# Group 1's first dense layer by seven products in all four units, under a new order of all operations (attention with squared ReLU, then two dense layers)

## The chip, the cores and the metric

The kernel runs on one core of one Trainium2 chip. The metric is the device time of one execution in microseconds (us). The kernel before took 365.93 us in the median of three runs (365.68 to 366.21). One execution was profiled: it took 365.47 us, and its span, from the first to the last instruction, is 363.7 us at a mean granted TensorE clock of 0.999.

## What is computed

```python
scores = (1 / sqrt(64)) * q @ k.T                  # 8 batches x 12 heads, 448 x 448, depth 64
attn_out = (max(scores, 0)**2 / 448) @ v           # per head: 448 x 64
x = attn_out as 3584 rows of 768                   # heads side by side
h = x @ w_in                                       # 3584 x 768 times 768 x 2048: first dense layer
g = h * sigmoid(1.702 * h)
out = g @ w_out                                    # 3584 x 2048 times 2048 x 768: second dense layer
```

Inputs and output are float32. Inside, matrix operands are float16 and sums are float32 in PSUM. The scale factors are held back and applied inside the GELU and at the output copies.

## The kernel before

**Attention.** The work is cut into 24 attention units of four heads of one batch (three units per batch). A unit's q and k are loaded, cast to float16 and transposed (the first six units by TensorE, the others by a DMA transpose). For each of seven blocks `j` of keys, `scores` (L143) issues four matmuls that run side by side in the four 64x64 quarters of the array and write two PSUM banks. `relu` (L156) copies each bank to SBUF with a ReLU, on ScalarE (L163) or VectorE (L161). `square` (L165) squares the two halves in one instruction, on ScalarE (L169) or VectorE (L88). `attn_v` (L173) multiplies by v in 28 matmuls. `xt_evac` (L189) copies the result to the transposed input of the dense layers, `xe` or `xo`.

**Dense layers.** The 3584 rows are taken in eight groups of 384 (even groups) and 512 (odd groups) rows. The first layer of a group gives sixteen tiles of 128 of the 2048 hidden columns. There are two ways to compute them:

- Plain: `m1` (L221) computes one tile `f` by six matmuls as wide as the group, two per call (words `f<g>.<f>.<r>`). Then `m1_gelu` (L233) reads PSUM on ScalarE and `m1_widen` (L238) scales into the float16 tile `ge`/`go` on GpSimd or VectorE.
- Seven products: `unit_product` (L269) handles a unit `i` of four hidden tiles at once. It splits weights and input into 2x2 blocks and needs seven block products in place of eight (a Strassen-Winograd scheme). Each product (word `u<g>.<i>.<n>`) is six matmuls of half the group's width. The sums of the input blocks (`t_sum`, L259, words `T`) are made once per group, those of the weight blocks (`s_sum`, L245, words `S`) once per unit for the whole kernel, both on VectorE. Two PSUM banks hold a unit. The first is copied out after products 0, 2 and 4 (`unit_snap`, L288, words `t`, on ScalarE or VectorE); the second is added to such a copy after products 1, 3 and 6 (`unit_add`, L295, words `b`, on VectorE). Four GELUs (`unit_gelu`, L299) and four scalings (`unit_widen`, L307) follow, each over two half tiles.

Group 0 is plain, groups 2 to 7 use seven products, and group 1 uses `m1` for hidden tiles 0 to 7 (the words `f1.0` to `f1.7`) and seven products for its units 2 and 3. The second layer (words `p`, `pair_product`, L375) uses seven products on pairs of row blocks and `single` (L399) on the odd block of the even groups; its block sums are the words `A` and `W` on VectorE. Stores go out on SyncE's queue.

**The order.** Nothing is scheduled at build time. The string `words` (L467 to L640) is a list of 1950 words, one per operation, written by a planner outside the kernel, and `do` (L441) issues them one after the other. Each engine takes its own operations in the order of this list. A suffix `:a`, `:d` or `:p` puts an operation on ScalarE, VectorE or GpSimd, and `@` names PSUM banks. Semaphores follow from the data and buffers.

The few lines that matter for the change:

```python
for i in (2 * r, 2 * r + 1):                                   # m1, L228
    nc.tensor.matmul(out=hp[g, f][:, 0:n], lhsT=w[:, i, fo:fo + 128],
                     rhs=xts[g][:, i, 0:n], start=i == 0, stop=i == NK - 1)
...
for t in range(2):                                             # unit_product, L269
    mm(hx[g, i, c][:, t * hn:(t + 1) * hn],
       lambda j: a[:, j, t * 128:(t + 1) * 128], lambda j: b[:, j, :], HK,
       n in (0, 1, 3) and t == 0)
```

All weight loads are DMAs issued by GpSimd (`jwa`, `jwb`, `jo`), as are the loads of v and of the first q and k; later q and k loads and transposes are on SyncE's queue.

Of the kernel before, what the change touches and what calls it, by code (L numbers as in the profile page):

```python
# [15 lines left out]
def kernel(  # L16
# [406 lines left out]
    with tc.manual_schedule():  # L423
# [35 lines left out]
        def zeros(e, p, n):  # L459
# [8 lines left out]
            "jq1 z13@0 z1 jk1 I jwb2 Lq0 Q0:a tq0@1 Lk0 jq2 K0:d tk0@2 eq0 ek0 jk2 tq1@3 eq1 "  # L468
            "s0.2@4.5 s0.3@6.7 tk1@0 r0.2.1 V0 r0.3.0 r0.3.1:d ek1 r0.2.0 s0.5@1.2 r0.5.0 s0.1@3.5 "
            "r0.1.0:d s0.0@6.7 r0.0.0 r0.5.1:d r0.1.1 jk3 s0.4@0.4 s0.6@1.3 r0.6.1:d r0.6.0 "  # L470
            "s1.0@6.2 r1.0.1 r1.0.0 r0.4.0 V1 r0.0.1:d s1.2@5.3 r0.4.1:d jq3 x0.6:a jwb0 r1.2.0 "
            "x0.5 s1.1@1.2 r1.1.1 x0.4 s1.5@6.0 r1.5.0:d x0.0 r1.5.1 jwa0 r1.2.1:d s1.3@7.4 x0.3 "
            "r1.1.0 x0.2 s1.4@5.2 x0.1:a tq2@6 x1.0 tk2@0 eq2 x1.5:a jk4 a0@3.1 ek2 r1.3.0 e0.1.0 "
            "jq4 s1.6@6.0 V2 jwa2 tk3@7 x1.1:a e0.0.0 r1.4.0 jwb1 r1.4.1:d ek3 s2.0@3.5 x1.4 "
            "e0.0.1:a tq3@2 jwa1 r1.3.1 x1.3 r2.0.1 jk5 s2.4@7.4 r1.6.0 r2.4.0 jq5 V3 e0.1.1 "
            "r2.4.1:d jwb3 s2.1@5.6 x1.2 r1.6.1 x1.6 s2.2@7.1 r2.0.0 a1@4.0 jwa3 r2.2.1 V4 r2.1.0 "
            "r2.2.0 r2.1.1 V5 x2.0 e1.0.0:a eq3 e1.1.0 s2.6@3.1 e1.0.1:a x2.1 jo1.0 r2.6.0 e1.1.1 "
            "s2.3@5.7 s2.5@6.2 r2.3.0 r2.3.1:d x2.2 r2.5.1 jo0.0 f0.3.0@4 f0.3.1 r2.6.1:d s3.3@3.0 "
            "s3.2@5.7 r3.2.1:d r3.3.1 r3.3.0 tk4@2 r2.5.0:d tq4@1 x2.3:a ek4 jo1.1 r3.2.0 x2.4 "
            "f0.2.0@7 x2.5:a x2.6 f0.2.1 s3.0@0.3 a2@6.2 r3.0.1 e2.0.1:a e2.1.0:a eq4 s3.1@5.3 "  # L480
            "r3.1.0 e2.1.1:a e2.0.0 jo0.1 r3.1.1:d x3.1 f0.1.0@1 f0.1.1 f0.1.2 x3.2 f0.3.2 r3.0.0 "
            "f0.2.2 g0.1 g0.3 v0.3:d f0.0.0@5 v0.1:d g0.2 s3.5@2.6 s3.6@3.0 r3.6.0 s3.4@1.4 r3.6.1 "
            "r3.4.1 r3.4.0:d f0.8.0@7 f0.8.1 f0.0.1 r3.5.1 r3.5.0:d f0.0.2 x3.4 v0.2 f0.8.2 "
            "s4.2@3.0 g0.0 r4.2.1:d x3.3:a s4.3@4.1 s4.1@6.2 r4.1.1 x3.5 r4.1.0 f0.6.0@5 f0.6.1 "
            "r4.3.0 x3.0 f0.6.2 g0.6 f0.4.0@0 f0.4.1 f0.4.2 g0.8 r4.3.1:d r4.2.0:d s4.4@2.6 "
            "r4.4.0:d tk5@4 x3.6 r4.4.1 tq5@5 g0.4 v0.4 s4.0@7.1 eq5:a ek5 s4.5@3.2 G3 a3@6.0 "
            "s5.6@5.4 r4.5.1 r4.0.0:d r4.5.0 x4.4 x4.2:a e3.0.0 s5.0@2.7 f0.7.0@3 r5.0.1:d r5.6.0:d "
            "r5.0.0 Lk6 f0.7.1 x4.1:a f0.10.0@6 r4.0.1 Lq6 f0.10.1 f0.10.2 g0.10 v0.10 f0.5.0@7 "
            "f0.5.1 f0.5.2 g0.5 K6:p e3.0.1:a Lk7 f0.7.2 f0.11.0@5 v0.6:d f0.11.1 r5.6.1 s5.1@2.1 "
            "r5.1.0 s4.6@6.7 f0.11.2 r5.1.1 f0.15.0@0 r4.6.0 v0.0:d x4.0 f0.15.1 x4.3 f0.15.2 g0.7 "  # L490
            "r4.6.1:d s5.4@4.2 x4.5 r5.4.1 x4.6 a4@1.6 r5.4.0:d s5.5@3.7 g0.11 s5.3@2.4 g0.15 "
            "e4.0.1:a s5.2@5.0 v0.15 r5.5.1:d x5.0:a f0.13.0@6 f0.13.1 f0.13.2 r5.5.0:d r5.3.0 x5.4 "
            "Rk6 x5.5:a V6 f0.9.0@7 S3.1 v0.8 e4.0.0 f0.9.1 r5.3.1 f0.14.0@3 v0.5 f1.4.0@2 f0.9.2 "
            "S3.2 f0.14.1 f0.14.2 g0.13 v0.7 V8 g0.9 r5.2.0:d f0.12.0@1 f0.12.1 S0.1 f0.12.2 V7 "
            "f1.1.0@4 v0.9 r5.2.1 v0.11 f1.4.1 f1.7.0@6 g0.14 v0.14 x5.2 f1.7.1 x5.3:a u1.3.0@7 "
            "x5.6 T1.1 x5.1:a a5@5.0 f1.1.1 g0.12 t1.3.0 Q6:d S1.1 e5.0.1:a u1.2.0@3 S2.1 Lq8 S2.2 "
            "f1.0.0@1 e5.0.0:a f1.1.2 S2.4 v0.12:d t1.2.0 f1.4.2 S1.2 T1.2 v0.13 S2.3 Rq6 g1.4 T1.4 "
            "A0.0.1@0 u1.2.1@0 b1.2.1 W0.1 f1.0.1 f1.3.0@5 f1.3.1 f1.3.2 W2.1 A0.0.3 f1.2.0@2 S3.3 "
            "u1.3.2 g1.1 g1.2.1 v1.1 f1.5.0@4 f1.5.1 v1.2.1 K7 f1.2.1 g1.3 f1.2.2 Lk8 W1.1 g1.2 "
            "f1.5.2 S3.4 A0.0.2@1 f1.7.2 g1.5 v1.2:d u1.2.2 v1.3 g1.7 f1.0.2 g1.0 v1.5 v1.4 t1.2.2 "  # L500
            "f1.6.0@5 t1.3.2 f1.6.1 T1.3 p0.0.0@2 W3.1 v1.0:d f1.6.2 u1.2.4 Q8:a t1.2.4 W0.2 u1.2.3 "
            "h0.0.0 v1.7:d W2.2 u1.3.4 W0.3 b1.2.3 g1.6 u1.2.5 W2.3 v1.6:d Lq7 g1.2.3 v1.2.3 "
            "s6.0@4.6 r6.0.0 W1.2 s6.2@1.5 u1.2.6 u1.3.1@4 r6.2.0:d Rk7 W3.2 b1.3.1 r6.0.1 Rq8 W3.3 "
            "W1.3 g1.2.5 s6.1@1.6 p0.0.1@3 r6.1.0 W0.4 t1.3.4 x6.0:a g1.3.1 u1.3.5 u1.3.3 r6.1.1:d "
            "l0.0.1 r6.2.1 p0.0.2 b1.2.6 x6.2:a b1.3.3 Q7:a Rq7 h0.0.2:d s6.5@1.6 r6.5.0:d r6.5.1 "
            "v1.3.1 s6.3@5.0 r6.3.1:d g1.3.5 K8:p x6.1:a v1.3.5 Lq9 Q9 u1.3.6 b1.3.6 g1.3.6 v1.3.6 "
            "Lk9 K9:p p0.0.4 h0.0.4 s6.4@1.6 r6.4.1 W3.4 r6.3.0 W2.4 r6.4.0 s6.6@0.7 r6.6.0 W1.4 "
            "A0.0.4 v1.2.5 p0.0.3 r6.6.1:d p0.0.5 x6.4 x6.5:a s7.2@4.6 l0.0.3 r7.2.0 r7.2.1 x6.3 "
            "Rk8 s7.0@5.1 r7.0.1:d r7.0.0 g1.2.6 l0.0.5 s7.1@0.7 r7.1.1:d p0.0.6 x6.6:a l0.0.6 Lq10 "
            "s7.3@4.6 A0.2.5@1 r7.1.0 r7.3.1 o0.1 r7.3.0:d a6@1.5 Lk11 e6.1.1 e6.1.0 e6.0.1:a "  # L510
            "s7.6@2.7 x7.2 r7.6.0 r7.6.1 Q10 e6.0.0:a s7.4@3.0 r7.4.0:d p1.0.0@6 s7.5@4.5 Rq9 "
            "r7.4.1 s8.1@2.7 r7.5.1 r8.1.0 s8.0@1.3 r8.0.1 x7.3 r7.5.0:d r8.0.0 x7.1:a Rk9 x7.6:a "
            "K11:p i0.2.0@0 s8.6@5.2 r8.6.0 x7.0 x7.5 r8.6.1 x8.6:a r8.1.1:d x7.4 n0.2.0 x8.1 "
            "a7@3.4 e7.1.0:a e7.0.0:a Lk10 Lq11 v1.2.6 s8.2@1.5 e7.1.1:a S1.4 s8.3@2.7 x8.0:a K10:p "
            "r8.2.0:d e7.0.1 A1.0.1@0 r8.2.1:d i0.2.1@0 r8.3.1 A1.0.3 r8.3.0 Rk11 A1.0.2@1 h1.0.0 "
            "n0.2.1:a p1.0.1@3 x8.3:a V9 o0.2 s8.4@1.4 s8.5@5.7 r8.4.0 r8.4.1 r8.5.1 x8.2 Q11 "
            "r8.5.0:d s9.2@2.0 Lk12 o0.0 V10 Rk10 r9.2.1:d V15 p1.0.2 x8.4 s9.1@1.4 r9.2.0 x8.5 "
            "s9.0@7.5 r9.1.0 a8@0.2 r9.1.1:d r9.0.0 s9.4@1.4 r9.0.1 s9.3@7.5 r9.3.1 l1.0.1 p1.0.3 "
            "e8.1.1:a u2.1.0@5 e8.0.1:a u2.0.0@2 S0.2 r9.3.0 S1.3 r9.4.1:d e8.0.0:a u2.1.1@7 t2.1.0 "
            "r9.4.0:d t2.0.0 T2.1 u2.2.0@4 e8.1.0 g1.3.3 T2.2 t2.2.0 T2.4 u2.0.2 T2.3 b2.1.1 "  # L520
            "u2.0.1@1 Lq12 g2.1.1 v1.3.3:d S0.3 u2.1.2 b2.0.1 u2.2.1@0 t2.0.2 t2.1.2 v2.1.1 g2.0.1 "
            "v2.0.1 u2.0.4 t2.0.4 A1.2.1@0 x9.1:a u2.1.4 u2.0.3 t2.1.4 u2.2.2 u2.1.3 S0.4 Rq11 "
            "b2.0.3 u2.0.6 g2.0.3 Rq10 b2.2.1 K12:p u2.0.5 b2.1.3 u2.1.6 g2.2.1 v2.2.1:d v2.0.3 "
            "g2.1.3 b2.0.6 u2.1.5 t2.2.2 v2.1.3:d Lk13 A1.0.4 u2.3.0@1 g2.0.5 b2.1.6 u2.2.4 "
            "t2.3.0:d g2.0.6 u2.3.1@2 g2.1.6 v2.0.5 b2.3.1 v2.0.6 u2.2.3 t2.2.4 g2.1.5 v2.1.6 "
            "g2.3.1 v2.1.5 b2.2.3 u2.3.2 t2.3.2 A1.2.2@1 x9.4:a h1.0.2:d u2.2.5 v2.3.1 u2.2.6 "
            "b2.2.6 u2.3.3 g2.2.5 Q12:a u2.3.4 p1.0.4 h1.0.4 v2.2.5 s9.5@7.5 g2.2.3 r9.5.0 g2.2.6 "
            "x9.3 t2.3.4:d s9.6@0.4 b2.3.3 u2.3.5 g2.3.5 u2.3.6 r9.5.1:d r9.6.1 K13:p p1.0.5 "
            "r9.6.0:d l1.0.3 Rk12 b2.3.6 x9.2 Lk15 l1.0.5 s10.3@7.1 r10.3.1 V13 K15:p s10.1@5.4 "
            "s10.0@0.2 r10.0.1 Rq12 p1.0.6 x9.6 r10.3.0:d r10.0.0 x10.0 r10.1.0 p1.2.0@6 r10.1.1:d "  # L530
            "x9.0:a l1.0.6 g2.3.6 h1.2.0 x9.5 s10.5@1.2 s11.1@7.0 r11.1.1 a9@5.4 r10.5.1 r10.5.0:d "
            "v2.2.6:d Lq14 o1.0 r11.1.0 A1.2.3 s10.2@3.0 s10.6@2.1 v2.3.5 r10.6.0 r10.2.0 r10.2.1 "
            "r10.6.1:d p1.2.1@7 e9.0.0 x10.3:a p1.2.2 s11.0@2.3 e9.0.1:a Q14 l1.2.1 o1.1 r11.0.1 "
            "s10.4@0.1 s11.3@5.4 x10.6 Lq13 A1.2.4 r11.0.0:d p1.2.3 r10.4.1 x10.1 h1.2.2 p1.2.4 "
            "r11.3.1 x10.5 r10.4.0 r11.3.0 x10.4 x10.2:a h1.2.4:d x11.3 l1.2.3 s11.2@3.2 x11.1 "
            "r11.2.0 r11.2.1 x11.2 Lk14 s12.2@1.4 v2.3.6 a10@0.5 s11.5@3.2 r12.2.0 r11.5.1 Rk13 "
            "Rq14 p1.2.6 e10.0.0 r12.2.1 x11.0:a r11.5.0:d l1.2.6 v2.2.3:d e10.0.1:a g2.3.3 "
# [133 lines left out]
```

## Time and profile before

| | us |
|---|---|
| median of three runs (lowest, highest) | 365.93 (365.68, 366.21) |
| profiled execution | 365.47 |
| its span | 363.7 |
| TensorE (PE) busy | 355.3 |
| VectorE (DVE) busy | 309.6 |
| ScalarE (ACT) busy | 283.2 |
| GpSimd (POOL) busy | 123.4 |
| PE, first to last matmul | 1.16 to 359.6 |

Busy time is the union of an engine's instructions. The duration of a matmul in the trace includes its way through the array, which overlaps the next one, so the time from one start to the next is the better measure of what a matmul costs; the chain of waits shows it, since it merges runs of equal matmuls. The same holds in part for ScalarE and VectorE: the next instruction begins some 0.09 us before the recorded end of the one in front of it. L numbers are lines of the kernel; operations issued through helpers appear under the helper's line (L88 for every two-input VectorE operation, L79 and L83 for copies, L203 for matmuls issued through `mm`).

### The profile page before, as it was taken

How to read it: one execution, taken by the hardware profiler on the slowest of the kernel's cores; microseconds unless marked ns; L12 is line 12 of the kernel's file. 1: busy time of each engine (PE TensorE's matmuls, PEld its weight loads, DVE VectorE, ACT ScalarE, POOL GpSimd, SP SyncE). 2: the span in 40 equal slices, each digit the busy share in tenths (PEclk: the TensorE clock that was granted, in tenths of full speed). 3: DMA queues.
4: the chain of work that ended last, by engine and by line, in shares of the span. 5: the costliest groups of instructions: out<-in, count | busy, mean ns of one | idle time of the engine just before them, and what ended most of it. 6: DMA issues, size and time to landing. Idle time of an engine off the chain costs nothing.

```text
span 363.7 us, 9020 instructions
## 1 busy us (share of the span) xinstructions
PE 355.3 (98%) x3562; PEld 231.8 (64%) x3562; DVE 309.6 (85%) x577; ACT 283.2 (78%) x550; POOL 123.4 (34%) x171
## 2 busy tenths in 40 slices
PE   8899999999999999999999999999999999999995
PEld 4445555655579555885569655787558755687763
DVE  3998999799899998988999799978897999775672
ACT  3998995799989888988997899588996598362410
POOL 5655174425526240254243251145202221021300
PEclk9999999999999999999999999999999999999999
DMA  8999999959898789458995599515590031110315
GB/s 193 188 205 205 238 230 203 203 57 268 178 219 171 136 254 172 135 103 187 195 193 114 126 186 213 133 51 104 99 198 8 1 88 43 45 45 2 87 36 141
DMA packets 65227, 51.39 MB, mean 141 GB/s; under 512 B 35744, under 2 KB 61856, under 8 KB 65184
## 3 DMA queue, kind: packets, MB, share of 16 engines
q1 hardware_dynamic: 48256, 36.32, 42.3%
q0 software_dynamic: 16608, 14.09, 26.1%
q8 instruction: 28, 0.46, 0.5%
q10 hardware_dynamic: 320, 0.39, 0.3%
q14 instruction: 15, 0.12, 0.1%
HBM read 45.61 MB, written 11.01 MB: 156 GB/s over the span
## 4 chain that ended last, share of the span: by engine, by line
PE 87%; ACT 5%; DVE 5%; DMA 1%; issue 1%; SPq 0%; ACTq 0%
PE ox L203 29%; PE hx L203 29%; PE sc L150 9%; PE av L181 8%; PE ht L228 7%; PE os L203 4%; ACT at L163 3%; DVE at L161 1%; DMA kst<-in_k_dram 1%; ACT at L169 1%; DVE at L88 1%; ACT xe L79 1%; DVE asum L88 1%; PE tr L131 1%; DVE xe L83 0%
## 5 line engine op out<-in xcount | busy, mean ns | idle before, releaser
L163 ACT ACTIVATE at<-sc 128x448 f16<-128x448 f32 x228 | 111.5, 574 | 13.6 <-PE sc L150 12.2
L169 ACT ACTIVATE at<-at 128x896 f16<-128x896 f16 x72 | 68.6, 967 | 0.4
L161 DVE TENSOR_SCALAR at<-sc 128x448 f16<-128x448 f32 x108 | 64.4, 615 | 5.1 <-PE sc L150 4.6
L88 DVE TENSOR_TENSOR at<-at 128x896 f16<-128x896 f16 x96 | 61.4, 657 | 3.2 <-ACT at L163 2.7
L203 PEld LDWEIGHTS <-win 128*128 128x128 f16 x624 | 56.7, 98 | 8.6 <-issue 2.4
L217 POOL TENSOR_SCALAR go<-gf 128x512 f16<-128x512 f32 x48 | 35.9, 747 | 71.2 <-ACT gf L214 57.5
L88 DVE TENSOR_TENSOR gf<-hx,gf 128x512 f32<-128x512 f32 (+1 forms) x78 | 47.7, 624 | 14.3 <-PE hx L203 9.6
L214 ACT ACTIVATE gf<-gf 128x512 f32<-128x512 f32 (+1 forms) x78 | 44.5, 581 | 15.2 <-DVE gf L88 15.0
L150 PE MATMUL sc<-qT,kT 64*64 64x448 f16 x672 | 51.7, 359 | 1.7 <-ACT at L163 0.7
L217 POOL TENSOR_SCALAR ge<-gf 128x384 f16<-128x384 f32 x47 | 29.4, 626 | 65.7 <-ACT gf L214 63.7
L203 PE MATMUL ox<-wout,go 128*128 128x384 f16 x256 | 46.1, 326 | 0.0
L203 PEld LDWEIGHTS <-winS 128*128 128x128 f16 x468 | 42.5, 98 | 5.5 <-issue 1.6
L203 PEld LDWEIGHTS <-go 128*128 128x128 f16 x320 | 30.1, 98 | 22.4 <-issue 4.8
L181 PE MATMUL av<-at,v 64*64 64x448 f16 x672 | 36.6, 350 | 0.3
L203 PE MATMUL hx<-T,winS 128*128 128x256 f16 (+1 forms) x312 | 36.8, 260 | 0.0
L203 PEld LDWEIGHTS <-ge 128*128 128x128 f16 x256 | 24.2, 98 | 17.4 <-issue 3.4
L150 PEld LDWEIGHTS <-kT 64*64 64x64 f16 x672 | 18.0, 105 | 26.8 <-issue 21.5
L203 PE MATMUL ox<-wT,asum 128*128 128x384 f16 x192 | 34.9, 326 | 0.0
L79 ACT ACTIVATE gf<-hx 128x512 f32<-128x512 f32 (+1 forms) x50 | 26.3, 542 | 11.0 <-PE hx L203 7.6
L203 PE MATMUL hx<-xo,win 128*128 128x256 f16 x252 | 32.1, 273 | 0.0
L203 PEld LDWEIGHTS <-asum 128*128 128x128 f16 x224 | 21.2, 98 | 16.1 <-issue 2.3
L181 PEld LDWEIGHTS <-v 64*64 64x64 f16 x672 | 20.5, 107 | 11.9 <-issue 2.1
(77 smaller groups left out, 472.7 us busy)
## 6 DMA issues: line engine op xcount, KB each, us to landing
out_dram<-osb SPq DMA_DIRECT2D x52, 192.0 KB, 3.1
qst<-in_q_dram SPq DMA_DIRECT2D x19, 448.0 KB, 4.1
kst<-in_k_dram SPq DMA_DIRECT2D x19, 448.0 KB, 5.0
v<-in_v_dram POOLq DMA_DIRECT2D x24, 224.0 KB, 6.3
win<-in_moe_w_in_dram POOLq DMA_DIRECT2D x8, 384.0 KB, 10.7
wout<-in_moe_w_out_dram POOLq DMA_DIRECT2D x4, 768.0 KB, 22.3
q<-in_q_dram POOLq DMA_DIRECT2D x5, 224.0 KB, 7.6
k<-in_k_dram POOLq DMA_DIRECT2D x5, 224.0 KB, 6.7
```

What stands on the lines that cost most here:

```text
L79: nc.scalar.activation(out=o, in_=i, func=AF.Copy)
L88: eng[e].tensor_tensor(out=o, in0=x, in1=y, op=op)
L131: nc.tensor.matmul(out=ps[64 * a:64 * a + 64, j * 128:(j + 1) * 128], lhsT=x[:, a, 64 * j:64 * j + 64], rhs=ident[:, :], is_transpose=True)
L150: nc.tensor.matmul(out=sc[a][c, 0:S], lhsT=st["kT"][r, j, c], rhs=st["qT"][r, :, c], start=True, stop=True)
L161: nc.vector.tensor_scalar(out=o, in0=i, scalar1=0.0, scalar2=None, op0=ALU.max)
L163: nc.scalar.activation(out=o, in_=i, func=AF.Relu)
L169: nc.scalar.activation(out=at, in_=at, func=AF.Square)
L181: nc.tensor.matmul(out=av[s][64 * a:64 * a + 64, 0:S], lhsT=v16[r, a, 64 * j:64 * j + 64], rhs=at[r, a, :], start=(j == 0), stop=(j == J - 1))
L203: nc.tensor.matmul(out=o, lhsT=lhs(i), rhs=rhs(i), start=start and i == 0, stop=i == n - 1, skip_group_check=True)
L214: nc.scalar.activation(out=o, in_=i, func=AF.Gelu_apprx_sigmoid, scale=1.0 / SC)
L217: eng[e].tensor_scalar(out=o, in0=i, scalar1=SC, scalar2=1.0, op0=ALU.mult, op1=ALU.mult)
L228: nc.tensor.matmul(out=hp[g, f][:, 0:n], lhsT=w[:, i, fo:fo + 128], rhs=xts[g][:, i, 0:n], start=i == 0, stop=i == NK - 1)
```

## The change

The words `f1.0` to `f1.7`, with their eight GELUs and eight scalings, are removed. Units 0 and 1 of group 1 are added by `unit_product`: 14 words `u1.0.*` and `u1.1.*`, six words `t`, six words `b`, eight GELUs and eight scalings. No function of the kernel changes, and no DMA is added or removed. The order of all words is new, and so are the choice of engine for operations that can go to more than one engine and the PSUM banks. The list has 1952 words in place of 1950. Two pieces of it, before (-) and after (+), where group 1 starts:

```diff
-            "Rk6 x5.5:a V6 f0.9.0@7 S3.1 v0.8 e4.0.0 f0.9.1 r5.3.1 f0.14.0@3 v0.5 f1.4.0@2 f0.9.2 "
...
-            "f1.0.0@1 e5.0.0:a f1.1.2 S2.4 v0.12:d t1.2.0 f1.4.2 S1.2 T1.2 v0.13 S2.3 Rq6 g1.4 T1.4 "
-            "A0.0.1@0 u1.2.1@0 b1.2.1 W0.1 f1.0.1 f1.3.0@5 f1.3.1 f1.3.2 W2.1 A0.0.3 f1.2.0@2 S3.3 "
...
+            "x5.6:a u1.0.0@6 a5@3.5 Q6:a v0.8 v0.11 T1.1 f0.12.2 e4.0.1:a v0.1:d g0.15 t1.0.0 K6 "
+            "S1.2 e5.0.1 u1.1.0@2 t1.1.0 u1.3.0@1 e5.0.0 u1.1.1@5 T1.2 u1.0.2 S2.3 t1.0.2 S1.4 "
+            "f0.13.2 u1.0.1@3 T1.3 v0.15 g0.13 u1.0.4 f0.14.1 t1.0.4 S3.2 S1.3 v0.13 b1.0.1 T1.4 "
+            "W0.1 u1.1.2 u1.0.3 Lk7 Lq8 u1.2.0@7 g1.0.1 v1.0.1 t1.1.2 u1.1.4 b1.1.1 g1.1.1 W2.1 "
...
```

Counted over the whole list, the choice of engine moves: ReLU copies 228 on ScalarE and 108 on VectorE before, 218 and 118 after; squares 72 and 96 before, 59 and 109 after; copies to the dense input 38 and 34 before, 44 and 28 after; copies after products of units (`t`) 50 and 28 before, 63 and 21 after; copies to the output (`h`, `n`) 24 and 20 before, 32 and 12 after; evacuations of the TensorE transposes of k 0 and 6 before, 3 and 3 after; casts of q and k on GpSimd 24 before and 19 after. In scalings, GpSimd has 95 before and 94 after. The order starts with k's load ahead of q's on SyncE, with the first k cast and q cast both on VectorE, and with v's first load ahead of the building of the identity matrix on GpSimd. All sums `S0.*` and `S1.*` of the weight blocks of units 0 and 1 now stand ahead of group 1's products or among the first of them; before, `S0.2` to `S0.4`, `S1.3` and `S1.4` stood 220 to 390 words later, close to group 2's first products.

## Prediction

> **What bounds the kernel now.** I read the page's busy shares and slices first, then the chain of waits, then windows over the first 127 us, then VectorE's timeline.
>
> ```profile
> PE 355.3 (98%) x3562; PEld 231.8 (64%) x3562; DVE 309.6 (85%) x577; ACT 283.2 (78%) x550; POOL 123.4 (34%) x171
> ...
> PE   8899999999999999999999999999999999999995
> ```
>
> TensorE is busy in every slice but the ends. A busy matmul row alone proves little, so I look at starts, in the chain of waits:
>
> ```profile
> 62.64 2.59 PE ht L228 x12
> ...
> 68.91 2.62 PE hx L203 x24
> ...
> 80.34 0.50 PE sc L150 x8
> 80.84 2.71 PE ox L203 x16
> ...
> 344.01 15.61 PE ox L203 x96
> 359.65 0.56 DVE osb L396
> ```
>
> The columns are start, length, what. 2.59/12 = 0.216 us for 512 columns, 2.62/24 = 0.109 for 256, 15.61/96 = 0.163 for 384: matmuls follow each other at the array's rate. Behind scores, 16 of 384 columns take 2.71 in place of 2.60: a change between the quartered and the full array costs about 0.1. Comparing every start with these rates, I find 118 such changes (11.0 us), 10.4 us of other waits and slow starts before 31 us, and 0.4 us from there to the last matmul at 359.6. So TensorE sets the end, and a matmul removed after 31 us shortens the run, if nobody else becomes late.
>
> Who could become late is shown by the windows (length, then busy PE, PEld, DVE, ACT, POOL):
>
> ```profile
> 16.00:40.00 24.00, 22.95 (x322) 12.57 (x319) 22.35 (x46) 22.98 (x51) 13.28 (x19) 1.00 1.25 205
> 40.00:55.00 15.00, 14.97 (x134) 8.18 (x126) 13.88 (x25) 14.21 (x28) 8.22 (x11) 1.00 1.24 240
> 55.00:70.00 15.00, 15.00 (x113) 8.73 (x111) 12.96 (x26) 9.70 (x17) 7.52 (x8) 1.00 1.14 193
> 70.00:86.00 16.00, 16.00 (x144) 9.42 (x146) 15.73 (x31) 15.10 (x29) 5.04 (x7) 1.00 0.73 145
> 86.00:103.00 17.00, 16.79 (x192) 8.94 (x186) 16.01 (x28) 16.12 (x33) 8.71 (x10) 1.00 0.91 208
> 103.00:127.00 24.00, 24.00 (x275) 18.99 (x271) 22.46 (x47) 20.90 (x45) 8.30 (x12) 1.00 0.90 171
> ```
>
> VectorE is busy 58.6 of the 63 us from 40 to 103, where group 1 is computed. That is where the change adds to it. Its timeline shows how it behaves:
>
> ```profile
> 29.82 0.56 DVE L83 CAST xe<-av 128x384 f16<-128x384 f32 x1 [0.64 <-ACT xo L79]
> ...
> 67.00 0.79 DVE L88 TENSOR_TENSOR xo<-xo 128x768 f16<-128x768 f16 x1 [1.48 <-PE ht L228]
> ...
> 76.49 1.27 DVE L88 TENSOR_TENSOR gf<-hx,gf 128x512 f32<-128x512 f32 x2
> ...
> 92.87 0.56 DVE L85 TENSOR_SCALAR osb<-os 128x384 f32<-128x384 f32 x1 [0.46 <-PE os L203]
> ```
>
> From 67.0 to 92.9 its only gap over 0.12 us is one of 0.17: with a backlog it runs through. Elsewhere it waits for ScalarE (0.64) or TensorE (1.48).
>
> **What the Trainium skill says.** "TensorE: Matmul & The Clock Gate", section Back-to-back issue gap, gives N/2.4 + 2.5 ns: 216 and 109 ns for 512 and 256 columns. The trace agrees. The same section's 131 ns for 512 columns in a stream with weight loads is not seen here. "PSUM — Partial Sum Buffer", section PSUM bank collisions, wants two engines kept off one bank; the 0.64 above is VectorE waiting until ScalarE has read the same `av`. "SBUF — State Buffer", section Who interferes with whom: a VectorE instruction with two SBUF inputs contends with GpSimd's reads. That fits the squares here: mean 657 ns, but 0.61 undisturbed.
>
> **The change part by part.**
>
> *TensorE.* Removed: 8 tiles x 6 = 48 matmuls of 512 columns, 48 x 0.216 = 10.36 us. Added: 14 products x 6 = 84 of 256, 84 x 0.109 = 9.17. Net -1.19 us. The built program confirms the count: 72 more PE rows, 36 matmuls with their weight loads. A weight load takes 98 ns and lies under a matmul of 109, as for the 24 above. Changes between quartered and full array, counted in both lists: 118 and 118, so 0.
>
> *ScalarE.* Eight GELUs from `ht` (594 ns) become eight from `hx` or in place (591 and 628): +0.2. The copies after products are six more, put at about 0.5 start to start: +3. The new choice of engines takes about as much away (10 ReLUs at 0.43, 13 squares at 0.86 leave; copies and evacuations come). By my sum, start to start, ScalarE goes from 269.7 to 270.0.
>
> *VectorE.* Six additions at 0.61 (two took 1.27, the last with its tail of 0.09): +3.7. Ten ReLUs and 13 squares at 0.54 to 0.57: +12.8. Copies and evacuations given to ScalarE, less two casts taken over: about -9.4. Sum 298.6 to 305.7, +7.1. Hidden by TensorE in total (343 us), but not everywhere, see below.
>
> *GpSimd, SyncE, DMA.* Five casts fewer on GpSimd, the same DMAs, the same total of scalings. On SyncE's queue k's first load now passes q's; on GpSimd's, v's first load passes the identity matrix (0.73 us later; first needed by a transpose near 5.0 us, ready by about 4.2). The first score needs both q and k, so it starts at 7.4 to 7.5 as now. I cost this at 0, from -0.5 to +0.5: start-up to 31 us is shared by VectorE and ScalarE, whose sums ahead of the fourth `attn_v` (a3) rise by 0.4 each, while the new order takes fewer of one unit's pieces in turns from the same `av` bank, where the two gaps of 0.6 before 31 us came from. The first plain tile has 13.2 us of TensorE's work ahead of it in both lists, with its weight loads issued as early. The tail, one addition and a store behind the last matmul, is the same.
>
> *The moved sums and the cover.* I counted VectorE's work standing in each list ahead of an `attn_v`, start to start (as a check, the count gives 10.05 us for the fully busy 80 to 90 us). Before: a3 31.7, a5 44.3, a7 80.5, a9 109.9. After: 32.1, 45.7, 85.2, 113.7. The excess of 4.7 at a7 is the six additions (3.7) and the weight sums `S` and squares drawn forward, less some ReLUs. TensorE's work ahead of a7 falls from 81.4 to 80.2. In the trace a7 starts at 92.98, and VectorE's first piece at 5.5: 87.4 us for 80.5 of work, 6.9 to spare. After, a7 could start at 91.8: 86.2 for 85.2, 1.0 to spare. At the products of group 1 (48 to 66 us) the same sum, taken for each word's last VectorE input, leaves 0.4 to 0.5; at a9 2.4 or more. So the cover is nearly gone from 48 to 95 us. A VectorE gap beyond the spare delays additions, which hold PSUM banks, and squares, for which `attn_v` waits; TensorE queues its products behind that wait, microsecond for microsecond.
>
> How long will the gaps be? Low end: 0.17 in 26 us of backlog, 0.6 over 87. High end: the 5 us of gaps that VectorE has before 93 us now. Much of the 5 came because VectorE was ahead (the 1.48 and 0.60 waits on TensorE), so I take 1.3, against a spare of 1.0: 0.3 us of new waits, with 0 and 4 as ends.
>
> *Sum.* The profiled execution took 365.47 (span 363.7 and 1.8 around it). 365.47 - 1.19 + 0.3 = 364.6. The median of the runs lies 0.46 above the profiled one, so 365.0.
>
> **The rivals.**
>
> *The gain is eaten (within 0.2%).* VectorE's gaps come to 2 or 3 us where 1.0 fits: 365.93 - 1.19 + 1.2 = 365.9. For it: before 31 us, where VectorE has no spare time even now, it still had two gaps of 0.6. Against it: 26 us without a gap.
>
> *VectorE becomes the bound (slower).* Place: 45 to 95 us. Price: each us of gap beyond the spare 1.0 is one us of run. It decides from 2.9 us of gaps (1.9 of new waits eats 1.19 and 0.7 more). With 4 us of gaps, most of today's: 365.93 - 1.19 + 3.0 = 367.7. For it: ScalarE is busy 55.1 of the 63 us from 40 to 103 and gets 2.4 more ahead of a8, and three full engines that wait for each other rarely stay full. Against it: VectorE at 98% from 70 to 86 us left TensorE without a gap.
>
> *Better start-up.* If the gaps of 0.6 at 23 and 30 us vanish and nothing else is late, 365.93 - 1.19 - 0.7 = 364.0.
>
> That the products are not exchanged is ruled out by the built program.
>
> **How the numbers follow.** The forecast, 365.0, stands for 364.2 to 365.2: 0.45. Better start-up, below 364.2: 0.05. Gain eaten, 365.2 to 366.7: 0.28. VectorE the bound, above 366.7: 0.22. A difference of 0.2% (0.73 us) is about what a measurement of this kernel can tell from no change, so faster 0.50, same 0.28, slower 0.22. The range from 364.2 to 367.1 leaves out 0.05 below and about 0.15 above.
>
> **What would show it.** Right: 84 matmuls of 256 columns more among `hx`, no `ht` of 512; the chain with TensorE from about 31 us on; VectorE above 95% busy from 40 to 95 us, its gaps there under 1.5 us; TensorE's waits after 31 us under 1 us. Wrong: several waits of TensorE for VectorE between 45 and 105 us, 2 us or more in sum; or start-up waits different from 10.4 us by more than 0.5; or the changes between array modes dearer or cheaper than 0.1 each. A late stage with new waits after 127 us, where VectorE has 5 us and more to spare, would mean that my count missed another resource.

## The result and the profile after

| us | before | after |
|---|---|---|
| median of the runs beside each other (lowest, highest) | 366.07 (365.68, 366.63), 4 runs | 363.74 (363.23, 364.18), 4 runs |
| ratio, 95% interval | | 0.9935, 0.9916 to 0.9954 |
| profiled execution | 365.47 | 364.18 |
| span | 363.7 | 362.4 |
| last matmul ends | 359.61 | 358.12 |
| VectorE, ScalarE, GpSimd busy | 309.6, 283.2, 123.4 | 309.1, 284.9, 111.8 |

Forecast were 365.0 and 364.6 for the profiled execution. The direction was right, and the gain is more than twice the one forecast: 2.33 us in the medians instead of 0.93. The profiled executions differ by 1.29 only, so the first question was whether the rest is chance.

The head of the page of after; the chain of waits of after, with start, length and what; and the windows of after (length, then busy PE, PEld, DVE, ACT, POOL):

```profile
PE 352.5 (97%) x3598; PEld 236.0 (65%) x3598; DVE 309.1 (85%) x585; ACT 284.9 (79%) x560; POOL 111.8 (31%) x165
...
PE   8789999999999999999999999999999999999995
```

```profile
37.27 0.88 POOL wout L415
38.22 0.52 POOL ge L217
38.76 0.50 ACT gf L214
39.30 1.52 PE av L181 x28
41.20 2.06 PE ht L228 x12
...
67.87 3.93 PE hx L203 x36
...
342.52 15.61 PE ox L203 x96
358.15 0.56 DVE osb L396
```

```profile
40.00:55.00 15.00, 15.00 (x173) 8.48 (x165) 14.17 (x28) 14.41 (x31) 4.36 (x8) 1.00 1.27 229
55.00:70.00 15.00, 15.00 (x134) 12.69 (x131) 14.68 (x30) 11.71 (x22) 4.65 (x7) 1.00 0.86 156
70.00:86.00 16.00, 16.00 (x149) 9.42 (x150) 15.63 (x29) 15.95 (x32) 6.24 (x8) 1.00 0.83 164
86.00:103.00 17.00, 17.00 (x190) 8.99 (x183) 16.17 (x31) 16.76 (x35) 7.78 (x9) 1.00 1.01 223
```

3.93/36 is 0.109: the added products run at the rate assumed. From 40 to 103 us VectorE is busy 60.7 us (58.6 before) and ScalarE 58.8 (55.1 before), and TensorE has no gap. So VectorE did get fuller, as forecast, and no wait came of it. The one long wait of TensorE after 31 us is at 39.3, where the chain runs from GpSimd over ScalarE to `av`.

**One profile was not enough.** I took two more of each kernel. Here is TensorE's account, each start compared with the rate of the matmul before it (0.216, 0.163, 0.109 us for 512, 384, 256 columns). Mode changes (from the quartered to the full array or back, 0.093 us each) are taken out; a small negative sum means that matmuls run slightly faster than the rate assumed.

| us | before, three profiles | mean | after, three profiles | mean |
|---|---|---|---|---|
| execution | 365.47, 365.73, 366.27 | 365.82 | 364.18, 363.25, 363.38 | 363.60 |
| matmuls at their rates | 336.39 | | 335.20 | |
| mode changes (118) | 10.97 | | 10.97 | |
| waits up to 10 us | 3.50, 3.52, 3.78 | 3.60 | 4.39, 3.82, 3.80 | 4.00 |
| waits 10 to 30 | 6.86, 7.17, 6.60 | 6.88 | 6.00, 5.46, 5.46 | 5.64 |
| waits 30 to 45 | -0.09, 0.48, 0.46 | 0.28 | 0.82, 1.02, 0.85 | 0.90 |
| waits 45 to 110 | 0.87, 0.31, 1.12 | 0.77 | 0.01, 0.10, 0.09 | 0.07 |
| waits from 110 | -0.58, -0.56, -0.56 | -0.57 | -0.95, -0.96, -0.67 | -0.86 |
| span after the last matmul | 4.08, 4.08, 4.10 | 4.09 | 4.28, 4.25, 4.25 | 4.26 |

The means differ by 2.22 us: 1.19 of matmuls, 1.21 of waits (0.84 before 30 us, 0.70 at 45 to 110 and 0.29 later, less 0.62 that come new at 30 to 45), less 0.17 in the tail, the span after the last matmul. That agrees with the medians. The first profile of before was a lucky execution, and the first of after an unlucky one (its first score started at 8.0 us instead of 7.5). The edges of the rows cut through one wait: before waits 0.50 us at about 30 us in all three profiles, and in the first it is counted a row higher. In the second profile of before the granted clock was 0.5 for 3.4 us from 14.5 us on; what TensorE lost by that stands among its waits from 10 to 30 us.

### The profile page after: what moved, and what is told of

It is laid out like the page before. It is cut to its first block, busy times and chain, and to the rows that moved or that the text cites. A ratio compares the mean times of both kernels' runs of the same rounds, so it can differ in the third digit from the quotient of the medians.

```text
span 362.4 us, 9114 instructions
## 1 busy us (share of the span) xinstructions
PE 352.5 (97%) x3598; PEld 236.0 (65%) x3598; DVE 309.1 (85%) x585; ACT 284.9 (79%) x560; POOL 111.8 (31%) x165
## 4 chain that ended last, share of the span: by engine, by line
PE 90%; DMA 5%; DVE 2%; POOL 1%; issue 0%; ACT 0%
PE hx L203 32%; PE ox L203 31%; PE sc L150 9%; PE av L181 8%; PE os L203 6%; DMA q<-in_q_dram 3%; PE ht L228 3%; DMA k<-in_k_dram 2%; PE zp L463 1%; PE tr L131 1%; DVE at L88 1%; POOL wout L415 0%; DVE at L161 0%; POOL q L104 0%; POOL v L104 0%
## 5 line engine op out<-in xcount | busy, mean ns | idle before, releaser
L163 ACT ACTIVATE at<-sc 128x448 f16<-128x448 f32 x218 | 108.2, 567 | 10.7 <-PE sc L150 9.9
L161 DVE TENSOR_SCALAR at<-sc 128x448 f16<-128x448 f32 x118 | 69.5, 614 | 3.6 <-PE sc L150 3.2
L203 PEld LDWEIGHTS <-win 128*128 128x128 f16 x672 | 61.5, 98 | 8.4 <-issue 1.8
L88 DVE TENSOR_TENSOR at<-at 128x896 f16<-128x896 f16 x109 | 65.9, 633 | 0.9 <-ACT at L163 0.2
L217 POOL TENSOR_SCALAR go<-gf 128x512 f16<-128x512 f32 x42 | 28.2, 671 | 109.9 <-ACT gf L214 108.3
L88 DVE TENSOR_TENSOR gf<-hx,gf 128x512 f32<-128x512 f32 (+1 forms) x84 | 51.6, 627 | 11.0 <-ACT gf L79 7.9
L169 ACT ACTIVATE at<-at 128x896 f16<-128x896 f16 x59 | 56.5, 974 | 1.1 <-DVE at L161 0.8
L203 PEld LDWEIGHTS <-winS 128*128 128x128 f16 x504 | 46.1, 98 | 5.5 <-issue 0.9
L79 ACT ACTIVATE gf<-hx 128x512 f32<-128x512 f32 (+1 forms) x63 | 34.5, 554 | 18.5 <-PE hx L203 15.0
L203 PE MATMUL hx<-xo,win 128*128 128x256 f16 x288 | 35.9, 273 | 0.0
```

The lines of the kernel that those rows point to most:

```text
L79: nc.scalar.activation(out=o, in_=i, func=AF.Copy)
L88: eng[e].tensor_tensor(out=o, in0=x, in1=y, op=op)
L161: nc.vector.tensor_scalar(out=o, in0=i, scalar1=0.0, scalar2=None, op0=ALU.max)
L163: nc.scalar.activation(out=o, in_=i, func=AF.Relu)
L169: nc.scalar.activation(out=at, in_=at, func=AF.Square)
L203: nc.tensor.matmul(out=o, lhsT=lhs(i), rhs=rhs(i), start=start and i == 0, stop=i == n - 1, skip_group_check=True)
```

## The experiments

**Both kernels again.** No edit.

> The unchanged kernel before, for a second profiled execution and more times. Theory A (the change saves only TensorE's 1.2 us, and the first profiled execution of before, 365.47 against a median of 366.07, was merely a lucky one): ratio 1.000; the new profiled execution takes 366 or more, and its excess over 365.47 lies in waits of TensorE before 31 us, where the work waits for the first loads (11 to 11.5 us in place of 10.4). Theory B (the offset of about 0.5 us between profiled execution and median is a property of being profiled): the profiled execution is again about 365.5 while the timed ones are 366.

> The unchanged kernel after. Theory A: with ten and more executions of both kernels on one chip the ratio comes nearer to what the profiles show, 364.18/365.47 = 0.9965, say 0.995 to 0.997. Theory C (the new order saves another 1 us in most executions, apart from TensorE's 1.2 us): the ratio stays at 0.9935, and the profiled execution is near 363.5, with TensorE's waits before 31 us about 0.7 us below the 10.4 of the first profile.

Measured: before again 366.44 us (ratio 1.000, 0.9984 to 1.0015), after again 364.30 (0.9933, 0.9913 to 0.9953). The gain is not chance: theory A, that only TensorE's 1.2 us counts, falls. The third profiles:

> Before once more, for a third profile only. If the median of 366.5 over 73 executions is typical, the profiled execution should show some 0.5 to 1 us more in waits than the first two (10.8 and 11.0 us net of the mode changes): either before 32 us, where loads land, or at 85 to 106 us, where the sums for the second layer's products are late in two relatives of this kernel. If all profiles come out at 365.5 to 365.8, a profiled execution is simply faster than others.

> After once more, for a third profile only: TensorE's waits net of mode changes between 9.6 and 10.5 us as in the first two, with none after 41 us, and a tail of 4.3 us; time 363.3 to 364.3.

Measured: 366.27 and 363.38; their parts stand in the table above. The third profile of before has 0.8 us more waits at 45 to 110 us than the second, by one wait that ends at 100.8 us. VectorE, then GpSimd, then TensorE in that profile:

```profile
98.02 1.08 DVE L88 TENSOR_TENSOR go<-go 128x1024 f16<-128x1024 f16 x1
99.03 1.75 DVE L88 TENSOR_TENSOR asum<-asum,go 128x1024 f16<-128x1024 f16 x1
```

```profile
99.28 0.94 POOL L83 CAST q<-qst 128x896 f16<-128x896 f32 x1
```

```profile
100.83 1.47 PE L203 MATMUL ox<-wT,asum 128*128 128x384 f16 x8 [0.79 <-DVE asum L88]
```

The sum takes 1.75 us beside the cast and 0.68 elsewhere, and the product behind it waits.

**Start and rest apart.** A list of words can be cut: the first words of one order, and behind them the remaining words of the other order.

```diff
 newstart_plain: words[:254] of after (without S), then the rest of before, with f1.0 to f1.7
 oldstart_seven: words[:176] of before, then the rest of after, with u1.0 and u1.1
```

> The first 254 words of the new order (up to about 47 us, without the weight sums S) and behind them the words of before in their order, with group 1's hidden tiles 0 to 7 plain: the new start without the exchange. Theory C (after gains 2.3 us: 1.2 by the exchange and about 1 by a better start): -0.7 to -1.4 us, TensorE's waits before 32 us at 9.3 to 9.7 us. Theory A (only the exchange counts): 0, ratio 1.000. The seam between the two lists, where nine attention blocks have gone to other engines than the rest of the list was made for, could cost some tenths, not gain.

> The first 176 words of before (up to about 32 us) and behind them the words of after in their order, with seven products in all units of group 1: the exchange and the new order from there on, without the new start. Theory C: -1.2 us (-0.7 to -1.5 with the seam), TensorE's waits before 32 us as before at 10.4 to 11.2. Theory A: -1.2 as well, but then after itself has nothing that this kernel lacks, and its -2.3 would have to come back here.

Measured: the new start with the plain rest takes 367.43 us (1.0019, 1.0003 to 1.0036), the old start with the new rest 364.38 (0.9946, 0.9930 to 0.9962). So nearly the whole gain lies behind 32 us, and the new start alone is worth nothing. (The seams add two mode changes to the first kernel and take two from the second, 0.2 us each way.) The account says why. The new start does save waits from 10 to 30 us (5.97 against 6.88), but at 39 us it pays 1.3 us back. With the old rest behind it, the waits at 45 to 110 us are 1.61; with the new rest behind the old start they are 0.04. My theory C, a better start, was wrong in its place.

**The exchange by itself.** The order of before is kept up to 31 to 38 us and from about 110 us on; the 40 words of the eight plain tiles (the first expectation says sixteen by mistake) are replaced by the 42 words of units 0 and 1, and the sums `S` and `T` they need are drawn forward. The first try departs from before at 38 us, earlier than its expectation says; the second and third change the engine of 45 and 51 operations besides.

```diff
-... g0.1 g0.3 v0.3:d f0.0.0@5 v0.1:d g0.2 ...
+... g0.1 g0.3 v0.3:d f0.0.0@5 S3.1 v0.1:d g0.2 ...
...
-... f1.0.0@1 e5.0.0:a f1.1.2 S2.4 v0.12:d t1.2.0 f1.4.2 S1.2 T1.2 ...
+... e5.0.0:a T1.2 u1.0.1@6 v0.12:d u1.0.2 t1.0.2 u1.2.1@1 T1.4 v0.13 ...
```

> The exchange of products alone: the list of before up to 51 us and from 95 us on with its choice of engines, the sixteen plain tiles' words f1.0 to f1.7 replaced by units 0 and 1 of group 1, with the copies on ScalarE and the scalings on GpSimd, and the weight and input sums that these need drawn forward. Theory A (TensorE's saving is what counts): -1.2 us, up to -0.7 where the hand-made placement leaves a wait; ratio 0.997 to 0.998. Theory C (the new order of everything else brings about half of the gain): the same -1.2 at most, so that after stays 1 us ahead of it. Theory D (VectorE has no room for six additions and the early sums): no gain or slower, with waits of TensorE for VectorE between 50 and 95 us.

> The exchange again in the order of before, now with no weight sum ahead of its weights' arrival (the first try made VectorE wait 4.7 us for a transfer), and with the choice of engine changed for 45 copies, squares and scalings between 31 and 105 us so that VectorE finds room. Start up to 31 us and everything from 110 us on are those of before. If the exchange alone carries its gain: -1.2 us with a perfect order, -0.4 to -0.8 with this one made by hand. If VectorE is the limit between 50 and 95 us: 0 to +2, with TensorE's waits there for VectorE.

> The exchange in the order of before for the third time, now also with no sum of second-layer weights ahead of its weights' arrival (that was what cost the second try 2.6 us at 59.8 us), and with fewer scalings of group 1 beside VectorE's two-input sums. The start up to 34 us and everything from 114 us on are those of before; 51 operations in between change their engine. Theory (matmul time alone): with no new waits -1.2 us, 365.3; a hand-made order may leave waits of 1 to 1.5 us, so 365.2 to 366.8, with TensorE's last matmul 1.2 us earlier than its waits would put it. Rival (the exchange costs VectorE time that before's order does not have, whatever the placement): over 368, with waits of TensorE for VectorE between 50 and 106 us.

Measured: 379.49 us (1.0352, 1.0326 to 1.0378), 376.81 (1.0288, 1.0241 to 1.0336) and 370.03 (1.0104, 1.0079 to 1.0128). The first two were spoilt by my own placement. This is VectorE in the first: a sum of weights that have not landed, and everything queued behind it,

```profile
38.30 0.56 DVE L88 TENSOR_TENSOR winS<-win 128x768 f16<-128x768 f16 x1 [4.66 <-DMA win<-in_moe_w_in_dram]
```

and in the second a sum of second-layer weights, likewise:

```profile
58.12 0.82 DVE L88 TENSOR_TENSOR wout<-wout,wout 128x768 f16<-128x768 f16 x1 [3.19 <-DMA wout<-in_moe_w_out_dram]
```

The third is free of both, and it is the telling one. Its products of 256 columns are 84 more than before's, and they start 0.109 us apart, as forecast; so the exchange saves its 1.2 us of matmul time here too. Six more mode changes take back 0.56. And at 45 to 110 us it has about 4.7 us of waits where before has 0.8, with VectorE full; these are its windows:

```profile
55.00:70.00 15.00, 14.14 (x135) 10.89 (x133) 14.70 (x26) 11.35 (x22) 6.48 (x10) 1.00 1.16 197
70.00:86.00 16.00, 15.76 (x133) 9.61 (x133) 16.00 (x28) 14.82 (x29) 6.27 (x7) 1.00 0.58 141
86.00:103.00 17.00, 16.18 (x160) 8.84 (x156) 16.40 (x29) 13.90 (x30) 8.54 (x9) 1.00 0.75 174
```

VectorE (third number) has no idle microsecond from 70 to 86 us, and TensorE (first) waits. Part of VectorE's time is lost beside GpSimd. First VectorE, then GpSimd, then TensorE of this kernel:

```profile
84.93 1.28 DVE L88 TENSOR_TENSOR wT<-wout,wT 128x768 f16<-128x768 f16 x1
86.13 1.41 DVE L88 TENSOR_TENSOR asum<-ge 128x1024 f16<-128x1024 f16 x1
```

```profile
84.39 1.41 POOL L83 CAST q<-qst 128x896 f16<-128x896 f32 x1 [4.06 <-DMA qst<-in_q_dram]
85.75 1.26 POOL L83 CAST k<-kst 128x896 f16<-128x896 f32 x1
```

```profile
88.07 1.46 PE L203 MATMUL ox<-wout,ge 128*128 128x384 f16 x8 [0.64 <-DVE osb L396]
```

The two sums take 0.55 and 0.68 undisturbed. So in this order the exchange is the rival "VectorE becomes the bound", by its mechanism, though at twice its size (+3.7 us; +1.8 was put down for it). Among the orders that were run, the order decides the sign of the change. That the exchange must lose in the order of before is not shown: three placements by hand gave +13, +10 and +3.7 us, and a better one may exist.

**How much room VectorE has.** Six products of 128x768 that nobody reads, one every 3 us from 48 to 63 us, 3.4 us in all:

```diff
+        def load_test(e, p):
+            w = win[3][:, 0:HK, 0:256]
+            tt(wT[2][:, 0:HK, 0:256], w, w, ALU.mult)
+        two["y"] = load_test
```

> After with six more VectorE products of 128x768 (0.57 us each, 3.4 us in all, results never read) spread from 48 to 63 us. My forecast put VectorE's spare time there at 1.0 us less 1.3 us of gaps: then the run grows by about 3.4 us (3.1 to 3.7), with TensorE's waits for VectorE between 50 and 95 us. If VectorE has spare time that I did not count (the copies and the casts before it are ahead of need), the run grows by less than 2 us; if it has the 3 us that before had, by under 0.5.

> Before with the six extra VectorE products of 128x768 (3.4 us) from 48 to 63 us that cost after 1.5 us. My forecast put VectorE's spare time in before at 6.9 us, up to the seventh attention unit: the load of 3.4 fits, so under 0.5 us; after lost 1.5 us because it has 3 to 4 us less. If before loses 1.5 us as well, the loss is local to each insertion (a chain that waits 0.57 us longer) and says nothing of spare time.

Measured: after takes 365.87 us with the load (0.9984 of before, 0.9967 to 1.0001), 1.6 more than its 364.30 beside it; before takes 370.62 (1.0096, 1.0064 to 1.0127), 4.0 more. Before's six executions fall into two groups: four lose about 4 us, two only 1.3 and 1.7; the profile is one of the four. After's waits at 45 to 110 us rise from 0.1 to 1.8 us. Of 3.4 us of load after took some 1.8 without loss: that is its room at these places, where the forecast, 1.0 less gaps of 1.3, had left none. Before, for which I had counted 6.9, lost more than the whole load in most executions. In its profile VectorE has a backlog from 64 to 76 us; a scaling in it frees a buffer late, a GELU on ScalarE waits for the buffer, and a product waits for the copy behind that GELU. The load's products read two SBUF inputs themselves, so part of their cost may be that they stretch GpSimd's work; that was not separated. The waits of TensorE in before with the load, in us in total, times, longest:

```profile
PE hx L203 <- ACT gf L79: 2.4, 1, 2.4
PE ox L203 <- DVE asum L88: 1.1, 1, 1.1
```

**Which feature of before's order is at fault?** Three attempts, each taking one away: five scalings of group 1 from GpSimd to VectorE; the cast of the third profile moved behind two transfers' issue; the in-place subtraction `T1.3`, for which VectorE idles 1.48 us at 67 us, moved behind ready work.

```diff
-v1.1 v1.2.1 v1.3 v1.5 v1.4
+v1.1:d v1.2.1:d v1.3:d v1.5:d v1.4:d
```

```diff
-V9 ... Q11 ... V10 ... V15 p1.0.2
+V9 ... V10 ... V15 Q11 p1.0.2
```

```diff
-f1.6.1 T1.3 p0.0.0@2 W3.1 v1.0:d f1.6.2 u1.2.4 Q8:a t1.2.4 W0.2
+f1.6.1 p0.0.0@2 W3.1 v1.0:d W0.2 T1.3 f1.6.2 u1.2.4 Q8:a t1.2.4
```

> Before with five scalings of group 1 (57 to 68 us) on VectorE in place of GpSimd, where four of them take 1.4 us each beside VectorE's two-input operations in place of 0.65. Theory (the order of before is brittle there: GELUs wait up to 3.3 us for buffers that the slowed GpSimd frees, and in executions without a profile this now and then reaches TensorE): the median falls by 0.3 to 0.8 us, towards the 365.6 of the profiles. Rival (GpSimd's slowness there hides behind TensorE in all executions): 0, or slower by up to 1 us since VectorE has 1.7 us more to do.

> Before with one cast (q of attention unit 11, some 0.95 us on GpSimd) behind two transfers' issue instead of between them, so that it starts near 101.3 us instead of 98.9 to 100.8. In the third profile of before, and in its relative with the new start, this cast begins just ahead of VectorE's sum for group 1's second layer (128x1024, two inputs), which then takes 1.75 us in place of 0.68, and TensorE waits 0.86 to 0.96 us for it; in the first two profiles VectorE comes first and there is no such wait. Theory (which of the two comes first varies between executions, and costs before up to 0.9 us in part of them): no wait at 98 to 103 us in the profile, and a median 0.2 to 0.6 us below before's. Rival (a rare case that does not reach the median): 0.

> Before with VectorE's in-place subtraction T1.3, which must wait until the plain products have read its input (1.48 us of idle VectorE at 67 us in all three profiles of before), moved behind three operations that are ready, so that they fill the gap. Theory (this wait exists only because group 1 is part plain and part seven products; it eats the VectorE time that is missing at 95 to 106 us): VectorE's sums at 96 to 99 us come up to 1.3 us earlier, the waits of TensorE at 85 to 106 us (0.8, 0.3 and 1.1 us in three profiles) go, and the median falls by 0.3 to 0.8 us. Rival (VectorE catches up before 95 us anyway, since it waits for the products there): 0.

Measured: 366.10 (0.9996, 0.9986 to 1.0005), 366.35 (0.9993, 0.9981 to 1.0005) and 366.83 us (1.000, 0.9983 to 1.0016). Each time the rival was right: nothing. The waits at 45 to 110 us are 1.48, 1.48 and 1.71 in these profiles. With the cast moved, the sum at 99.2 us takes its 0.68, but another sum beside another cast takes 1.37 at 86.1, and TensorE still waits at 89 and 102 us. None of the three alone is the cause. (The expectation for the scalings takes a mean for the single case: of the four, one takes 3.28 us and the others 0.62 to 0.83; more on it at the end.)

**Two small changes to after.** With tile 3's scaling of group 0 on VectorE, and with the products of the last pair turned round so that the store `o7.0` leaves earlier:

```diff
-jo1.1 r3.6.0 f0.4.0@7 f0.4.1 f0.4.2 s4.2@1.0 jo0.1 G3 g0.8 v0.3 g0.4
+jo1.1 r3.6.0 f0.4.0@7 f0.4.1 f0.4.2 s4.2@1.0 jo0.1 G3 g0.8 v0.3:d g0.4
...
-p7.2.2 p7.2.3 h7.2.2 p7.2.4 p7.0.6 ... l7.2.3 q7.3.1.0 A7.2.4 q7.3.1.1:a l7.0.6 p7.2.5 ... o7.0
+p7.2.2 p7.0.6 h7.2.2 p7.2.4 l7.0.6 o7.0 ... A7.2.4 p7.2.3 l7.2.3 q7.3.1.0 q7.3.1.1:a p7.2.5 ...
```

> After with two small changes of its order. One scaling of group 0 (tile 3, about 35 us) goes from GpSimd, where it stands behind the issue of two weight loads, to VectorE, so that the GELU behind it gets its buffer in time; and the products of the last row pair are turned round so that the big store of the tile before leaves 1.3 us earlier. Theory: TensorE's wait of 0.77 and 0.99 us at 39 us in two profiles of after goes, -0.4 to -0.9 us, and the tail after the last matmul shrinks from 4.3 to 4.1 us; 363.0 to 363.7 where after has a median of 364.2. Rival: VectorE, full from 33 to 47 us, passes the scaling's 0.28 us on and a new wait appears there: 364.0 to 364.5.

Measured: 362.97 us, 0.9917 of before (0.9898 to 0.9935); after had 364.30 and 363.74 (0.9933 and 0.9935), on other occasions. The intervals overlap, so the times alone do not prove a gain; the trace shows what went. In its profile (362.09) the wait at 39 us is gone (0.00 at 30 to 45 us), the waits at 45 to 110 stay at 0.03, and the tail is 4.12. TensorE there, with no idle time before `av`:

```profile
37.01 0.57 PE L150 MATMUL sc<-qT,kT 64*64 64x448 f16 x8
37.41 1.49 PE L181 MATMUL av<-at,v 64*64 64x448 f16 x28
```

The cause of that wait is seen in the third profile of after. GpSimd first, then ScalarE, then TensorE:

```profile
36.21 0.87 POOL L415 DMA_DIRECT2D wout<-in_moe_w_out_dram  x1 [0.41 <-DMA v<-in_v_dram]
37.16 1.88 POOL L217 TENSOR_SCALAR ge<-gf 128x384 f16<-128x384 f32 x3
```

```profile
37.70 0.49 ACT L214 ACTIVATE gf<-ht 128x384 f32<-128x384 f32 x1 [0.89 <-POOL ge L217]
```

```profile
38.24 1.52 PE L181 MATMUL av<-at,v 64*64 64x448 f16 x28 [0.67 <-ACT gf L214]
```

A weight load that waits for an earlier transfer holds GpSimd's queue; the scaling behind it frees a buffer late; the GELU waits for the buffer, and `attn_v` waits for the GELU, because it takes over the PSUM bank that the GELU reads (`f0.6.0@3`, `a3@3.6`). The wait varies with the landing of the earlier transfers: 0.77, 0.99, 0.83 in the three profiles, and nothing in after with the load, where the four weight loads are issued one behind another without a wait.

## Why the prediction was right or wrong

- **TensorE, -1.19 us, mode changes 0: right.** After has 84 products of 256 columns more and none of 512, they start 0.109 us apart (3.93/36), and there are 118 changes in all three profiles.
- **Start-up 0, from -0.5 to +0.5: wrong up to 30 us.** Up to 30 us the waits fall by 0.84 on average (+0.40 before 10 us, -1.24 behind), and from 30 to 45 us they rise by 0.62. Taken together that is -0.22, no more than the range allowed, but by two misses that nearly cancel. The new wait at 39 us I had not seen at all: I went through GpSimd's queue for its casts and first loads, but not for the scalings that now stand behind the loads of the second layer's weights. The same chain would have been visible in the lists.
- **VectorE's room falls from 6.9 to 1.0 us: both numbers were wrong, and the comparison was the error.** VectorE's work grows about as forecast (+6.7 us by the spacing that its operations have undisturbed; +7.1 forecast), yet its busy time falls from 309.6 to 309.1 us: less of it is spent in stretched operations. For after I had assumed 1.3 us of lost VectorE time; from 40 to 95 us it lost 1.1 (time from start to start, less the sum of the durations used in the prediction). By that sum 1.0 of room would have been used up; the load found 1.8 more. For before I called the time up to a7 that VectorE did not work "to spare". It was lost: from 40 to 95 us 6.9 us by the same sum, of which 3.9 in gaps behind ScalarE and TensorE, and some in operations stretched beside GpSimd (1.5 us from 48 to 66 us; 0.3 in after). The load of 3.4 us shows that in most executions this time could not be used where the load was placed. The new order puts about 5 us more work into the same stretch by not losing it.
- **New waits +0.3: wrong, this is the term that failed.** Measured -0.70 at 45 to 110 us and -0.29 behind. I only asked what the change would make late, and took before's own waits there (0.3 us at 101 in the first profile) as fixed and small. In all seven profiles with the old order of that stretch and plain products they are 0.3 to 1.7 us; in the five profiles of after, its version with two small changes and the old start with the new rest they are 0.0 to 0.1. This term is nearly the whole miss: between the means the forecast is 1.33 us short, and -0.99 in place of +0.3 is 1.29 of it.
- **The tail, no change: off by 0.17 us**; the store of the tile before stands nearer to the last one, and with it moved forward the tail is 4.12.
- **The profiled execution, 364.6: 364.18 measured, by luck.** An early loss of loads made up for waits that vanished. The mean of three is 363.60. Adding 0.46 for the median fits before (366.07 and 366.56 against 365.82) and after (363.74 and 364.30 against 363.60) on the whole; but profiles of one kernel lie up to 0.9 us apart, and a sum made against one profile cannot be trusted to 0.4 us.
- **Announced signs.** VectorE above 95% busy from 40 to 95 us: 53.1 of 55 in the first profile, right; its gaps there under 1.5: 1.6 to 1.9, a little more. TensorE's waits after 31 us under 1 us: about right (0.8 to 1.0), at a place not named. Start-up waits that differ from 10.4 by more than 0.5 were a sign of being wrong: 10.4 in one profile, 9.3 in two.
- **The rivals.** "Better start-up" gave 364.0, about the right number for a cause that is only part of it. One gap that it named did shrink: VectorE's 0.64 at 30 us is 0.16 in after, and TensorE's wait there falls from 0.50 to 0.15. But the new wait at 39 us takes that back, and the kernel with the new start alone gains nothing. "VectorE the bound" is what the exchange does in the old order.

What was shown: the saved matmul time; the wait at 39 us and its cause; room of 1.8 us in after for the load as placed; and that the waits at 45 to 110 us go when the words behind 32 us are those of after. Left open: whether they go because of the order or because group 1's plain products are gone. Every kernel with the old order there and small waits had plain products, and the new rest was never run with plain products. Left open too is which feature of the old stretch makes it wait: taking three away one at a time changed nothing, and they were not taken away together.

## What to carry to other kernels

Idle time of a nearly full engine is spare only if something could have been placed in it; test it with a load before counting on it. When an edit comes with a whole new order, the edit and the order are two changes: here the edit, placed by hand in the old order, made the kernel 1% slower at best, and with a new order it was 0.65% faster. Make the sum against several profiles, not one, when the gain looked for is smaller than the spread of executions.

## What the runs showed of the hardware

- VectorE's sums of two SBUF inputs and GpSimd's casts and scalings stretch each other. In the profiles of before and after a sum of 128x1024 takes 0.68 to 1.75 us, a cast 0.92 to 1.45, a scaling of 128x512 0.61 to 3.28. The Trainium skill ("SBUF — State Buffer", section Who interferes with whom) says that a VectorE instruction with two SBUF inputs contends with a GpSimd instruction that reads SBUF, through a pair of ports that they share, and that the order of issue decides who blocks. The traces agree that one of the two is held up, but who it is can't be told from the recorded starts. In the first profile of before the sum starts at 98.60 and the cast at 98.86, and the cast is stretched (1.22); in the third they start at 99.03 and 99.28, and it is the sum. First VectorE, then GpSimd of the first profile, to be set against the lines shown above:

```profile
98.60 0.68 DVE L88 TENSOR_TENSOR asum<-asum,go 128x1024 f16<-128x1024 f16 x1
```

```profile
98.86 1.22 POOL L83 CAST q<-qst 128x896 f16<-128x896 f32 x1
```

- The hold can last through several sums. In all three profiles of before one scaling takes 3.28 us instead of 0.62, and VectorE runs five sums of two SBUF inputs back to back meanwhile, from 61.91 to 64.60 us. GpSimd, then the first and the last of the five, in the first profile:

```profile
61.80 3.28 POOL L217 TENSOR_SCALAR go<-gf 128x512 f16<-128x512 f32 x1 [0.76 <-ACT gf L214]
```

```profile
61.91 0.68 DVE L88 TENSOR_TENSOR ge<-ge 128x1024 f16<-128x1024 f16 x1
63.92 0.68 DVE L88 TENSOR_TENSOR asum<-asum,ge 128x1024 f16<-128x1024 f16 x1
```

  With that scaling on VectorE (the five scalings moved) the time did not change, so it cost nothing here by itself.
- Executions of the same program differ: 365.18 to 368.25 us in 14 of before. The profiles show three sources: which engine of a pair is held up; the landing of the first loads (first score at 7.5 or 8.0 us); and the granted clock. In the second profile of before it was 0.5 from 14.5 to 17.9 us, and the 28 matmuls of an `attn_v` took 2.37 us there; the 28 at 37.41 us shown above took 1.49:

```profile
16.12 2.37 PE L181 MATMUL av<-at,v 64*64 64x448 f16 x28
```

  How much each source adds to the spread was not measured.
